# First q and k quad loaded in fp32 over the hardware queues, all of v over GpSimd's queue, bias matmuls apart and one-bank first scores, in a fused attention and channel-mix kernel

## The chip, the cores and the metric

The kernel runs on one core of one Trainium2 chip. The metric is the device time of one execution in microseconds; for the kernel before it is the median of three runs, 227.96 us (227.42 to 228.73). The profile is of a further execution of the same program, which took 229.82 us.

The engines that work beside each other are TensorE (PE, with its weight loads as PEld), VectorE (DVE), ScalarE (ACT), GpSimd (POOL) and SyncE (SP). Each takes its instructions in the order in which they stand in its own list. DMAs are issued by SP and ACT (hardware queues) and by GpSimd (software queue).

## The reference

```python
scores = scale * np.matmul(q, k.transpose(0, 1, 3, 2))   # q, k, v: (8, 8, 576, 64)
rel = pos[:, None] - pos[None, :]
bias = slopes[:, None, None] * (-np.abs(rel).astype(np.float32))[None, :, :]
mask = (rel >= 0) & (rel < window)                       # window = 128
scores = np.where(mask, scores + bias[None], -1000000000.0)
attn = softmax(scores)
x = (attn @ v) with the heads side by side               # (8, 576, 512)
...
xk = mu_k * x + (1.0 - mu_k) * x_prev
xr = mu_r * x + (1.0 - mu_r) * x_prev
k = np.maximum(xk @ w_k, 0.0)                            # w_k: 512 x 1024
v = k * k @ w_v                                          # w_v: 1024 x 512
r = 1.0 / (1.0 + np.exp(-(xr @ w_r)))                    # w_r: 512 x 512
return (r * v).astype(np.float32)
```

`x_prev` is x shifted by one position within a batch. The lines on softmax and on x are shortened here.

## The kernel before

**Attention.** Each of the 8 batches has two *quads* of four heads. A quad of q or k is one load of 128 rows of 1152 values (`quad_load`, into `raw`); DVE transposes it in blocks of 32 x 32 into `qt` (`turn`, L902). `scores4` computes scores of four heads, with keys as rows, in two halves: half 0 holds the first 256 query columns of two key blocks, half 1 the rest (pieces of 256, 192 and 64 columns). Four matmuls of 32 rows each run beside each other (L933). ACT takes the exponential (L954) of two heads at a time, 1024 columns in a double bank of PSUM (`duo`, two of them), into `at`. For batches 1 to 7 DVE multiplies by a prepared mask (L968). For batch 0 the bias and the mask are instead added in PSUM by matmuls of `sid` (a scaled identity per head) with `dist` (L924), in the same planned step as the scores.

`attend` multiplies by v, which has a column of ones for the sum (L668; tiles `vs` and, for the last 64 positions, `tv`); DVE takes the reciprocal (L674) and DVE or ACT scales (L679, L685) into `xu`. For batches 0 to 2 PE transposes `xu` (L706) and ACT copies it to `xt` (L551); from batch 3 on a DMA transpose does this. `shift` forms the two mixes `xk` and `xr` on DVE (L732, L739). Batch 0 goes through attention in two parts (positions 0 to 255, then the rest), so that the channel mix can begin early.

**Channel mix.** For blocks of 256, 384 or 512 positions PE multiplies by `wk_sb` (L797), ACT takes the rectifier (L804), ACT or DVE the square (L768, L770); PE multiplies by `wr_sb` (L815) and ACT takes a tanh in place of the sigmoid (L822); PE multiplies by `wv_sb` (L831), and DVE joins the two and hands the tile to an output DMA (L836, L861). PSUM has, beside the two double banks, four single ones (`uno`), which the mix, the transposes and batch 0's attends share.

**Order.** The whole program is planned as a graph of steps. `Plan.run` goes through it with a duration for each step, and on each engine takes the ready step of lowest rank that gets its buffers. The rank comes from the tables `LEAD`, `SHIFT` and `NUDGE`, which hold numbers found by a search. The order found is then written out as each engine's fixed list.

**The start.** PE runs 90 warming matmuls (L637). SP and ACT each load one block of batch 0's v in fp32 into an output buffer (`v_first`, L544), and ACT and DVE cast one block each (L551). GpSimd's queue takes, in the order of `LOADS`, the first quad of k and q, the forming of `dist`, the second quad of k and q, half of w_k, the rest of v, the other half of w_k, and then batch 1 and the other weights. Its DMAs cast fp32 to bf16 on the way. A transpose waits for its quad; the scores wait for both transposes of their quad; batch 0's first four attends need the first two blocks of v. A one-off transpose on PE (L627) with a copy on DVE (L631) prepares mu.

Of the kernel before, what the change touches and what calls it, by code (L numbers as in the profile page):

```python
# [182 lines left out]
def kernel(  # L183
# [36 lines left out]
    LOADS = 'xyKVkabRcWw'  # L220
    XD = 4
    OTL = 3.5
    VHKB = 327
    BIAS = (0, 1)
    FIN = 384
# [9 lines left out]
    WAIT = 96.32  # L235
# [26 lines left out]
    tv_buf = many(NV, [128, H, W], BF16, "tv")  # L262
    at_buf = many(NA, [128, 2 * 1024 + 64], BF16, "at")
    rc_buf = many(NX, [128, 2, NJ], FP32, "rc")
# [34 lines left out]
    plan = Plan(dict(p2=2, p1=N1, pt=4 - N1, at=NA, xu=NX, vs=NV, cb=NC, qt=NT, xt=2, dl=2, dl0=4,  # L299
# [10 lines left out]
    def dve_t(n, fast=1):  # L310
# [4 lines left out]
        PE: (245.41, 104.68, 82.24, 280.97, 280.85, 383.85, 240.38, 304.14, 232.01, 250.0),  # L315
        ACT: (106.83, 31.51, -1.26, 283.31, -80.09, 110.86, -49.36, -66.59, 49.19, -329.22),
        DVE: (226.97, 54.51, 122.69, 32.62, 2.01, -18.69, -19.49, -68.72, -71.7, 53.31),
# [3 lines left out]
        PE: {(0, 0): 164.1, (3, 0): -101.36, (2, 0): 106.01, (1, 0): -253.38, (1, 1): -8.62, (1, 2): 168.96, ('p1', 'fxk'): -4.58, ('rl', 'fp1'): -124.01, ('frl',): 851.64, ('rs', 'fp1'): 412.51, ('p1', 'fkk'): 3.25, ('fkk',): -221.64, ('ot', 'fp1', 'frs'): -20.61, ('fp1', 'frs'): 251.26},  # L321
        ACT: {(0, 0): -193.01, (3, 0): -156.82, (2, 0): 30.74, (1, 0): -160.97, (1, 1): 250.14, (1, 2): 336.32, ('p1', 'fxk'): 2.22, ('rl', 'fp1'): 331.51, ('frl',): 234.49, ('rs', 'fp1'): -327.51, ('p1', 'fkk'): -152.67, ('fkk',): -200.74, ('ot', 'fp1', 'frs'): -427.51, ('fp1', 'frs'): 310.6},
        DVE: {(0, 0): 106.18, (3, 0): 52.28, (2, 0): 70.04, (1, 0): -243.69, (1, 1): -278.94, (1, 2): 50.14, ('p1', 'fxk'): 976.06, ('rl', 'fp1'): -340.74, ('frl',): 236.08, ('rs', 'fp1'): 888.24, ('p1', 'fkk'): 232.82, ('fkk',): -853.72, ('ot', 'fp1', 'frs'): -155.85, ('fp1', 'frs'): 44.72},
    }
    NUDGE = {
# [210 lines left out]
    def v_first(j, h, deps):  # L536
# [4 lines left out]
        def stage():  # L541
            return ot_buf[hs.idx].rearrange("p (h d) -> p h d", d=D)
# [520 lines left out]
```

## Time and profile before

| | us |
|---|---|
| median of three runs | 227.96 (227.42 to 228.73) |
| profiled execution, device time | 229.82 |
| its span, first to last instruction | 228.0 |
| PE busy in the span | 214.2 |
| DVE busy | 196.6 |
| ACT busy | 163.8 |
| GpSimd busy | 55.1 |

Each row of time order has the start in us, the busy time in us, engine, line, operation, tiles and their shapes; a bracket at the end says how long the engine was idle before and what ended this. Matmuls are pipelined, so a busy time of PE is not work at its peak rate. A DMA shows as the instruction that issues it; its landing is another number.

### The profile page before, as it was taken

What the parts mean: (1) busy time and instruction counts of PE and PEld (TensorE: products, weight loads), DVE (VectorE), ACT (ScalarE), POOL (GpSimd) and SP (SyncE); (2) the same over time, 40 slices, a digit from 0 to 9 for tenths busy, and PEclk for the clock granted to TensorE, in tenths of its full rate; (3) what the DMA queues carried; (4) which work ended last, traced back from release to release, by engine and by line L of the source; (5) the groups of instructions that cost most, each with busy time, mean ns of one, the idle gap of its engine ahead of it and who ended that gap; (6) DMA issues with size and microseconds to landing.
All of it is one profiled execution on the core that took longest, in us unless ns stands there. A gap on an engine that the chain in (4) does not pass through costs nothing.

```text
span 228.0 us, 5641 instructions
## 1 busy us (share of the span) xinstructions
PE 214.2 (94%) x2233; PEld 128.8 (56%) x2263; DVE 196.6 (86%) x376; ACT 163.8 (72%) x313; POOL 55.1 (24%) x85
## 2 busy tenths in 40 slices
PE   8847969999999999999999999999999999999994
PEld 8736647665656555445664555456555446446642
DVE  7856999999999999999999997999697988995332
ACT  6155899988999889596965997847794588417511
POOL 8627445472710000083007400380000000000000
PEclk9997997999999999999999999999999999999999
DMA  7999999999993211489947992699815331422023
GB/s 141 194 181 212 183 176 211 168 212 173 237 169 9 95 46 35 92 190 170 180 95 135 199 187 58 155 183 205 128 40 54 100 138 33 85 97 89 0 92 138
DMA packets 63993, 30.11 MB, mean 132 GB/s; under 512 B 52184, under 2 KB 55776, under 8 KB 63968
## 3 DMA queue, kind: packets, MB, share of 16 engines
q0 software_dynamic: 42672, 16.52, 65.0%
q1 hardware_dynamic: 20112, 12.92, 20.5%
q10 hardware_dynamic: 1184, 0.33, 0.7%
q8 instruction: 17, 0.28, 0.5%
q14 instruction: 8, 0.07, 0.1%
HBM read 33.56 MB, written 9.44 MB: 189 GB/s over the span
## 4 chain that ended last, share of the span: by engine, by line
PE 73%; ACT 10%; DMA 6%; DVE 5%; issue 2%; POOL 1%; POOLq 0%; SPq 0%; DVEq 0%
PE uno L831 25%; PE uno L797 23%; PE uno L815 10%; PE duo L668 7%; PE duo L933 6%; ACT at L954 6%; DMA raw<-in_q_dram 4%; DMA xt<-xu 2%; ACT rl L804 1%; ACT kk L768 1%; PE uno L706 1%; PE duo L924 1%; DVE xr L739 1%; DVE xu L679 1%; DVE at L968 1%
## 5 line engine op out<-in xcount | busy, mean ns | idle before, releaser
L954 ACT ACTIVATE at<-duo 128x1024 bf16<-128x1024 f32 x64 | 64.3, 1041 | 22.9 <-PE duo L933 22.9
L797 PE MATMUL uno<-xk,wk_sb 128*128 128x256 bf16 (+2 forms) x410 | 71.3, 314 | 2.3 <-ACT xt L551 0.8
L831 PE MATMUL uno<-wv_sb,kk 128*128 128x512 bf16 (+2 forms) x286 | 68.1, 373 | 0.7 <-issue 0.2
L804 ACT ACTIVATE rl<-uno 128x256 bf16<-128x256 f32 (+2 forms) x104 | 47.5, 482 | 15.5 <-PE uno L797 13.7
L797 PEld LDWEIGHTS <-wk_sb 128*128 128x128 bf16 x416 | 38.8, 98 | 25.9 <-issue 3.8
L831 PEld LDWEIGHTS <-kk 128*128 128x128 bf16 x296 | 27.8, 98 | 29.3 <-issue 0.9
L902 DVE STREAM_TRANSPOSE qt<-raw 128x576 f32<-128x576 f32 x32 | 38.9, 1239 | 2.6 <-DMA raw<-in_q_dram 1.7
L968 DVE TENSOR_TENSOR at<-at,mask 128x1024 bf16<-128x1024 bf16 x56 | 37.3, 676 | 1.2 <-ACT at L954 0.9
L822 ACT ACTIVATE rs<-uno 128x512 bf16<-128x512 f32 x36 | 22.2, 617 | 19.5 <-PE uno L815 19.5
L815 PE MATMUL uno<-wr_sb,xr 128*128 128x512 bf16 x130 | 35.2, 380 | 0.8 <-issue 0.2
L768 ACT ACTIVATE kk<-rl 128x256 bf16<-128x256 bf16 (+2 forms) x71 | 34.3, 514 | 0.6
L836 DVE SCALAR_TENSOR_TENSOR ot<-rs,uno 128x512 f32<-128x512 bf16 (+2 forms) x37 | 24.2, 661 | 7.2 <-PE uno L831 6.6
L513 POOL DMA_DIRECT2D vs<-in_v_dram x30 | 26.6, 906 | 5.6 <-DMA wv_sb<-in_moe_w_v_dram 2.0
L668 PEld LDWEIGHTS <-at 128*128 128x128 bf16 x576 | 21.9, 100 | 7.9 <-ACT at L954 3.1
L739 DVE SCALAR_TENSOR_TENSOR xk<-dl,mu_sb,xt 128x576 bf16<-128x576 bf16 (+1 forms) x32 | 24.6, 776 | 0.0
L739 DVE SCALAR_TENSOR_TENSOR xr<-dl,mu_sb,xt 128x576 bf16<-128x576 bf16 (+1 forms) x32 | 24.4, 771 | 0.0
L933 PE MATMUL duo<-qt 32*128 32x256 bf16 (+2 forms) x640 | 21.3, 254 | 2.3 <-DVE rc L674 1.1
L679 DVE TENSOR_TENSOR xu<-duo,rc 128x640 bf16<-128x640 f32 x28 | 22.3, 811 | 0.2
L933 PEld LDWEIGHTS <-qt 32*128 32x128 bf16 x640 | 13.8, 94 | 14.3 <-issue 12.6
L815 PEld LDWEIGHTS <-xr 128*128 128x128 bf16 x144 | 13.1, 98 | 14.5 <-issue 1.5
L668 PE MATMUL duo<-vs,at 128*128 128x65 bf16 x448 | 19.3, 197 | 0.5 <-DVE at L968 0.3
L595 POOL COPY gap<-xt 1x4 bf16<-1x4 bf16 x3 | 0.9, 289 | 68.0 <-DMA xt<-xu 68.0
(50 smaller groups left out, 137.4 us busy)
## 6 DMA issues: line engine op xcount, KB each, us to landing
out_dram<-ot SPq DMA_DIRECT2D x32, 256.0 KB, 2.4
raw<-in_k_dram POOLq DMA_DIRECT2D x16, 288.0 KB, 8.3
raw<-in_q_dram POOLq DMA_DIRECT2D x16, 288.0 KB, 7.4
vs<-in_v_dram POOLq DMA_DIRECT2D x30, 128.0 KB, 9.8
wk_sb<-in_moe_w_k_dram POOLq DMA_DIRECT2D x2, 512.0 KB, 12.1
wv_sb<-in_moe_w_v_dram POOLq DMA_DIRECT2D x2, 512.0 KB, 11.3
out_dram<-ot SPq DMA_DIRECT2D x6, 128.0 KB, 1.8
tv<-in_v_dram POOLq DMA_DIRECT2D x8, 64.0 KB, 9.3
```

Of the source, the lines that this page charges most:

```text
L513: return dma(POOL, 256, issue_t(1024), lambda e: nc.gpsimd.dma_start(out=vs_buf[h.idx][:, j, :, 0:D], in_=v[b, :, 128 * j:128 * j + 128].r ...
L668: nc.tensor.matmul(a[:, hl, t - t0], lhsT=at[:, lo:lo + 128], rhs=vs[:, u, 2 * g + hl, :] if u < NF else tvb[:, 2 * g + hl], start=(u == u ...
L739: lambda e: nc.vector.scalar_tensor_tensor(out=buf[hk.idx][:, g, e0 + c0:e0 + c1], in0=dls(), scalar=mu[:, g:g + 1], in1=xc(1), op0=ALU.mu ...
L768: nc.scalar.activation(out=out, in_=in_, func=AF.Square)
L797: nc.tensor.matmul(one(hp)[:, 0:n], lhsT=wk_sb[:, po, 128 * fo:128 * fo + 128], rhs=xk_buf[hx.idx][:, po, c0:c1], start=(po == 0), stop=(p ...
L804: a = op(ACT, act_t(n), [s], pr, lambda e, hp=hp, hr=hr: nc.scalar.activation(out=rl_buf[hr.idx][:, 0:n], in_=one(hp)[:, 0:n], func=AF.Rel ...
L815: nc.tensor.matmul(one(hp), lhsT=xr_buf[hx.idx][:, po, 128 * c:128 * c + 128], rhs=wr_sb[:, po], start=(po == 0), stop=(po == NPO - 1))
L831: nc.tensor.matmul(one(hv)[:, a:b], lhsT=kk_buf[hk.idx][:, fo, o:o + 128], rhs=wv_sb[:, fo, a:b], start=(fo == 0), stop=(fo == NFO - 1))
L902: nc.vector.transpose(out=qt_buf[hq.idx][:, S * i:S * i + S].rearrange("p s t -> p (s t)").bitcast(FP32) .rearrange("p (q t) -> p t q", t=TB),
L933: nc.tensor.matmul(two(hps[j // 2])[:, j % 2, c0:c0 + n], lhsT=qt[r:r + 32, S + 128 * u:S + 128 * u + 128, t], rhs=qt[r:r + 32, q0:q0 + n, t],
L954: lambda e, ah=ah, j=j: nc.scalar.activation(out=ah(), in_=two(hps[j]), func=AF.Exp, scale=float(scale)), (), [hps[j]])
L968: nc.vector.tensor_tensor(out=a, in0=a, in1=m, op=ALU.mult)
```

## The change

It does these things:

- The first quad of k and of q (batch 0, heads 0 to 3) is loaded in fp32, each in two halves of 64 rows, one over SP's and one over ACT's queue, into two `kk` buffers. Each tensor is then cast into `raw` in two halves of 576 columns, one by ACT and one by DVE.
- The first two blocks of v go over GpSimd's queue with the cast in the DMA, like the others. The queue's order is now: second quad of k and q, `dist`, two blocks of v, half of w_k, the rest of v, the other half of w_k, and then as before.
- The bias matmuls of batch 0 are a step of their own, which takes the PSUM banks and can run before q and k are there. Sixteen of them now stand in PE's list ahead of the first scores, eight of these among the warming matmuls.
- The scores of the second quad, first half, go to four single banks, with one exponential of 512 columns for each head in place of two of 1024.
- The reciprocals have six buffers that the plan hands out, in place of four in turn; the memsets of `tv` go by 32-bit elements; the count of hardware DMAs that decides how many of the last output tiles are written in two pieces becomes 63, so that one tile is split in place of three.
- The tables of ranks hold new numbers, so the order on every engine differs. DVE's list has four transposes in a row at the start (k one, k two, q one, q two), and the mask copies behind them. ACT has 18 in place of 12 small scalings of `xu`, and 76 in place of 71 squares.

```diff
-    LOADS = 'xyKVkabRcWw'
+    LOADS = 'ydvKVkabRcWw'
...
+    SINGLE = ((1, 0),)
...
-    rc_buf = many(NX, [128, 2, NJ], FP32, "rc")
+    rc_buf = many(6, [128, 2, NJ], FP32, "rc")
...
-            late(tv_buf[t][64:128], 0.0, 0.55)
+            late(tv_flat[t][64:128].bitcast(FP32), 0.0, 0.34)
...
-        x = dma(eng, VHKB, 0.46, lambda _: e.dma_start(
-            out=stage(), in_=v[0, :, 128 * j:128 * j + 128].rearrange("h p d -> p h d")),
-            [g], lat=(0.7, 0.7), kind="first")
...
+    def first_quads():
+        src = [(q, k)[i][0, 0:4].rearrange("h (p r) d -> (h p) (r d)", r=TB) for i in range(2)]
+        hs = [Hold("kk"), Hold("kk")]
...
+        for i in (1, 0):
+            for n, (eng, e) in enumerate(((SPE, nc.sync), (ACT, nc.scalar))):
+                rows = slice(64 * n, 64 * n + 64)
+                x[i, n] = dma(eng, QUADKB / 2, 0.46, lambda _, i=i, e=e, rows=rows: e.dma_start(
+                    out=stage(i)[rows], in_=src[i][rows]), [last["kk0"]], lat=(0.85, 0.75), kind="first")
+        res = {}
+        for i in (1, 0):
+            res[i] = [op(CAST, {ACT: act_t(TB * D / 2, True), DVE: dve_t(TB * D / 2)}, [x[i, 0], x[i, 1]],
+                         (0, 0, 0, 0, 5), lambda e, i=i, c=c: copy_any(
+                e, raw_buf[ch[0].idx][:, i, 0, c:c + TB * D // 2], stage(i)[:, c:c + TB * D // 2]),
+                (), [hs[i]]) for c in (0, TB * D // 2)]
...
+        elif what == "v":
+            vl[0].extend(v_load(0, j, vh[0], [gv[0]] + blank_v) for j in (0, 1))
...
-    n_hw = 39 + 2 + G * len(XO)
+    n_hw = 39 + 4 + G * len(XO)
...
+        single = b == 0 and (c, half) in SINGLE
+        hps = [Hold("p1") for _ in range(4)] if single else [Hold("p2"), Hold("p2")]
...
+        if bias:
+            deps = deps + [op(PE, 0.02 + sum(4 * mm(n) for _, _, n in pieces),
+                              [n_dist] + n_sid[4 * c:4 * c + 4], prio + (4,), emit_b, hps)]
...
+        for j, js in enumerate(((0,), (1,), (2,), (3,)) if single else ((0, 1), (2, 3))):
```

More of the change, by code (lines that the diff above doesn't have):

```diff
@@ L234 @@
     NO = 6
-    WAIT = 96.32
+    WAIT = 148.12
     COST = {'v': 1.15, 'tv': 0.58, 'w': 0.88}
@@ L314 @@
     LEAD = {
-        PE: (245.41, 104.68, 82.24, 280.97, 280.85, 383.85, 240.38, 304.14, 232.01, 250.0),
-        ACT: (106.83, 31.51, -1.26, 283.31, -80.09, 110.86, -49.36, -66.59, 49.19, -329.22),
-        DVE: (226.97, 54.51, 122.69, 32.62, 2.01, -18.69, -19.49, -68.72, -71.7, 53.31),
+        PE: (412.66, 13.74, 352.24, 231.79, 219.11, 455.43, 521.65, 19.38, 22.83, 259.26),
+        ACT: (120.42, -14.11, -11.49, 9.9, 64.54, -199.58, -184.6, -81.47, -112.35, -120.12),
+        DVE: (540.05, 6.52, 96.4, 66.38, -6.12, -94.16, -131.55, -24.25, 66.99, -77.3),
     }
@@ L442, in fab, with dma @@
         return x
-    def dma(queue, kb, issue, emit, deps=(), need=(), free=(), lat=(1.0, 0.9), flip=False, kind='x'):
+    def dma(queue, kb, issue, emit, deps=(), need=(), free=(), lat=(1.4, 0.9), flip=False, kind='x'):
         n = plan.add(queue, issue, 0.0, list(deps) + [last.get(queue)],
@@ L481 @@
     MSEG = ((256, 192), (448, 64))
+    for e in (PE, ACT, DVE, SPE, POOL):
+        last[e] = plan.add(e, 0.75, 0.0, [], (-1e10,))
     n_warm = dve_op(0.1, lambda e: nc.vector.memset(warm, 0.0), [], (0, -2))
@@ L555 @@
     gv = {0: virtual("vs", [vh[0]])}
-    vl[0] = [v_first(j, vh[0], [gv[0]] + blank_v) for j in range(2)]
+    ch, cl, gc = {}, {}, {}
+    ch[0] = Hold("cb")
+    gc[0] = virtual("cb", [ch[0]])
+    cl[0] = [first_quads()]
+    vl[0] = []
     plan.add(ACT, 1.28, 0.0, [last[ACT]], (-1e9,))
@@ L562, in load_step @@
     def load_step(what):
-        if what in "xy":
-            c = int(what == "y")
-            if c == 0:
-                ch[0] = Hold("cb")
-                cl[0] = []
-                gc[0] = virtual("cb", [ch[0]])
-            cl[0].append({i: quad_load(0, i, c, ch[0], gc[0]) for i in (1, 0)})
-            if c == 0:
-                n_w["d"] = pool_op(0.7, emit_cut, [n_ident])
+        if what == "y":
+            cl[0].append({i: [quad_load(0, i, 1, ch[0], gc[0])] for i in (1, 0)})
+        elif what == "d":
+            n_w["d"] = pool_op(0.7, emit_cut, [n_ident])
+        elif what == "v":
+            vl[0].extend(v_load(0, j, vh[0], [gv[0]] + blank_v) for j in (0, 1))
         elif what == "V":
@@ L603, in batch_load @@
             g_ = virtual("cb", [ch[b]])
-            cl[b] = [[quad_load(b, i, c, ch[b], g_) for i in range(2)] for c in range(2)]
+            cl[b] = [[[quad_load(b, i, c, ch[b], g_)] for i in range(2)] for c in range(2)]
         elif what == "c":
@@ L673, in emit_r @@
         def emit_r(e):
-            nc.vector.reciprocal(out=rc[:, :, 0:nt], in_=a5()[:, :, :, D])
+            nc.vector.reciprocal(out=rc_buf[hr.idx][:, :, 0:nt], in_=a5()[:, :, :, D])
         def emit_x(e):
+            rc = rc_buf[hr.idx]
             out_ = xo().rearrange("p t h d -> p h t d")
@@ L688, in attend @@
         a = op(PE, 0.029 * n_mm, deps, prio + (0,), emit, [hp], [ha, hv])
-        r = op(DVE, 0.2, [a], prio + (0,), emit_r)
+        r = op(DVE, 0.2, [a], prio + (0,), emit_r, [hr])
         on = XU(b, g)
         r = op(on, {ACT: 0.197 * 2 * nt, DVE: dve_t(2 * nt * D)}, [r], prio + (0,), emit_x,
-               [hx], [hp])
+               [hx], [hp, hr])
         return r, hx
@@ L906, in emit @@
                         "p (t w) -> p t w", w=32))
-            n = op(DVE, dve_t(S) + TURN, [cl[b][c][i], (n, 0.0)] + paced(b, 2 * c) + (n_pad if i else []),
+            n = op(DVE, dve_t(S) + TURN, cl[b][c][i] + [(n, 0.0)] + paced(b, 2 * c) + (n_pad if i else []),
                    (0, b, 0, 2 * c, 3), emit, [hq] if i else [], [ch[b]])
@@ L916, in scores4, with bank, emit_b @@
         a0 = BASE[pieces[0][0]] + pieces[0][1] - 128 * pieces[0][0]
-        hps = [Hold("p2"), Hold("p2")]
-        def emit(e):
-            qt = qt_buf[hq.idx]
-            for j in range(4 if bias else 0):
+        single = b == 0 and (c, half) in SINGLE
+        hps = [Hold("p1") for _ in range(4)] if single else [Hold("p2"), Hold("p2")]
+        prio = (0, b, 0, 2 * c + half) if b else (0, 0, half, 2 * c)
+        def bank(j):
+            return one(hps[j]) if single else two(hps[j // 2])[:, j % 2]
+        def emit_b(e):
+            for j in range(4):
                 for (u, q0, n) in pieces:
@@ L924, in emit @@
                     nc.tensor.matmul(
-                        two(hps[j // 2])[:, j % 2, c0:c0 + n], lhsT=sid[:, 4 * c + j],
+                        bank(j)[:, c0:c0 + n], lhsT=sid[:, 4 * c + j],
                         rhs=dist[:, 0:n], start=(u == pieces[0][0]), stop=False,
                         skip_group_check=True)
+        def emit(e):
+            qt = qt_buf[hq.idx]
             for (u, q0, n) in pieces:
@@ L933, in emit @@
                         nc.tensor.matmul(
-                            two(hps[j // 2])[:, j % 2, c0:c0 + n],
+                            bank(j)[:, c0:c0 + n],
                             lhsT=qt[r:r + 32, S + 128 * u:S + 128 * u + 128, t],
@@ L937, in emit, with ah @@
                             start=(t == 0 and not bias), stop=(t == 1), skip_group_check=True)
-        prio = (0, b, 0, 2 * c + half) if b else (0, 0, half, 2 * c)
-        dur = 0.02 + sum(2 * max(n / 2400 + .0025, .03) for _, _, n in pieces)
+        need = (has if half == 0 else []) + ([] if bias else hps)
         if bias:
-            dur += 0.1 + sum(4 * mm(n) for _, _, n in pieces)
-            deps = deps + [n_dist] + n_sid[4 * c:4 * c + 4]
-        s = op(PE, dur, deps, prio + (2,),
-               emit, (has if half == 0 else []) + hps, [hq])
-        s.rows = (128 if bias else 32, 32)
-        res = []
-        for j in range(2):
-            def ah(j=j):
-                return at_buf[has[j].idx][:, 0:2048].rearrange(
-                    "p (h c) -> p h c", h=2)[:, :, a0:a0 + 512]
-            x = op(ACT, act_t(1024), [s], prio + (2,),
+            deps = deps + [op(PE, 0.02 + sum(4 * mm(n) for _, _, n in pieces),
+                              [n_dist] + n_sid[4 * c:4 * c + 4], prio + (4,), emit_b, hps)]
+        s = op(PE, 0.02 + sum(2 * max(n / 2400 + .0025, .03) for _, _, n in pieces), deps, prio + (2,),
+               emit, need, [hq])
+        s.rows = (32, 32)
+        res = [[], []]
+        for j, js in enumerate(((0,), (1,), (2,), (3,)) if single else ((0, 1), (2, 3))):
+            w = 512 * len(js)
+            p = js[0] // 2
+            def ah(js=js, p=p):
+                return at_buf[has[p].idx][:, 0:2048].rearrange(
+                    "p (h c) -> p h c", h=2)[:, js[0] % 2:js[-1] % 2 + 1, a0:a0 + 512]
+            x = op(ACT, act_t(w), [s], prio + (2,),
                    lambda e, ah=ah, j=j: nc.scalar.activation(
-                out=ah(), in_=two(hps[j]), func=AF.Exp, scale=float(scale)), (), [hps[j]])
+                out=ah(), in_=one(hps[j])[:, None] if single else two(hps[j]),
+                func=AF.Exp, scale=float(scale)), (), [hps[j]])
             if bias:
-                res.append(x)
+                res[p].append(x)
                 continue
@@ L968, in emit_m @@
                 nc.vector.tensor_tensor(out=a, in0=a, in1=m, op=ALU.mult)
-            res.append(op(DVE, dve_t(1024, 2), [x, n_mask] + ([] if m0 == 0 else n_mcopy),
+            res[p].append(op(DVE, dve_t(1024, 2), [x, n_mask] + ([] if m0 == 0 else n_mcopy),
                           prio + (2,), emit_m))
@@ L982 @@
             prio = (0, 0, 0, g)
-            r, hx = attend(0, g, 0, 2, has[j], [m0[j]] + vl[0][0:2], prio)
+            r, hx = attend(0, g, 0, 2, has[j], m0[j] + vl[0][0:2], prio)
             xks[0, 0, g], xrs[0, 0, g] = out_t(0, g, 0, 2, hx, [r], prio, xh[0], xth[0], late)
@@ L991 @@
             prio = (0, 0, 1, g)
-            r, hx = attend(0, g, 2, NJ, has[j], [m0[j], m1[j]] + vl[0] + blank, prio)
+            r, hx = attend(0, g, 2, NJ, has[j], m0[j] + m1[j] + vl[0] + blank, prio)
             xks[0, 1, g], xrs[0, 1, g] = out_t(0, g, 2, NJ, hx, [r], prio, xh[0], xth[0])
@@ L1007 @@
                 prio = (0, b, 0, g)
-                r, hx = attend(b, g, 0, NJ, has[j], [m0[j], m1[j]] + vl[b], prio)
+                r, hx = attend(b, g, 0, NJ, has[j], m0[j] + m1[j] + vl[b], prio)
                 if b in XO:
```

29 lines of the change are left out of this document (12 added, 17 removed), and 139 rows, old and new, of the table NUDGE.

## The prediction

> **What bounds the kernel now.** I read the page first, then the busy time by stretch, then the first 27 us in order of time, because the change touches what is loaded and computed there.
>
> ```profile
> span 228.0 us, 5641 instructions
> ...
> PE 214.2 (94%) x2233; PEld 128.8 (56%) x2263; DVE 196.6 (86%) x376; ACT 163.8 (72%) x313; POOL 55.1 (24%) x85
> ```
>
> Busy time by stretch (columns: stretch, its length, busy us of PE, PEld, DVE, ACT and POOL with counts, TensorE clock, DMA share, GB/s):
>
> ```profile
> 12.00:18.00 6.00, 3.27 (x49) 2.26 (x50) 3.02 (x8) 3.54 (x6) 1.76 (x3) 0.92 1.74 184
> 18.00:24.00 6.00, 5.21 (x97) 4.14 (x95) 4.01 (x13) 2.60 (x5) 3.81 (x6) 0.79 1.13 208
> 24.00:30.00 6.00, 4.93 (x77) 3.51 (x79) 6.00 (x13) 6.00 (x13) 2.47 (x4) 1.00 1.98 172
> 30.00:36.00 6.00, 4.46 (x80) 3.29 (x73) 5.48 (x11) 6.00 (x16) 3.47 (x6) 0.84 1.56 193
> 36.00:42.00 6.00, 5.93 (x75) 3.87 (x74) 5.79 (x14) 5.98 (x18) 2.34 (x3) 0.87 1.32 199
> ...
> 60.00:80.00 20.00, 19.65 (x248) 12.33 (x248) 19.74 (x32) 19.16 (x39) 3.74 (x5) 1.00 0.83 111
> ...
> 200.00:216.00 16.00, 15.95 (x99) 9.54 (x99) 10.08 (x24) 8.52 (x19) 0.00 (x0) 1.00 0.18 67
> 216.00:228.00 12.00, 8.91 (x48) 4.32 (x47) 3.59 (x6) 1.19 (x2) 0.00 (x0) 1.00 0.31 109
> ```
>
> From 36 us to the end PE is the bound: 5.93 of 6, 19.65 of 20, 15.95 of 16. Its total work doesn't change, so what it fails to do early is what can be won or lost. Between 12 and 18 us it is busy for 3.27 of 6 us, and ACT for only 3.54: both wait. Between 24 and 36 us ACT is full (6.00 and 6.00) and PE gets 4.93 and 4.46, so there ACT sets the pace. The early rows say what is waited for:
>
> ```profile
> 0.74 0.49 ACTq L544 DMA_DIRECT2D ot<-in_v_dram  x1
> ...
> 4.93 1.80 POOL L513 DMA_DIRECT2D vs<-in_v_dram  x2
> ...
> 5.08 0.62 ACT L551 CAST vs<-ot 128x512 bf16<-128x512 f32 x1
> 5.25 0.86 DVE L551 CAST vs<-ot 128x512 bf16<-128x512 f32 x1
> ...
> 7.87 1.26 DVE L902 STREAM_TRANSPOSE qt<-raw 128x576 f32<-128x576 f32 x1 [0.69 <-DMA raw<-in_k_dram]
> ...
> 8.88 0.22 PE L627 MATMUL uno<-id,mu_row 8*128 8x8 f32 x1
> ...
> 9.27 1.26 DVE L902 STREAM_TRANSPOSE qt<-raw 128x576 f32<-128x576 f32 x1
> ...
> 10.37 0.17 DVE L631 COPY mu_sb<-uno 128x8 f32<-128x8 f32 x1
> 10.58 0.64 PE L933 MATMUL duo<-qt 32*128 32x256 bf16 x16 [0.50 <-DVE mu_sb L631]
> ...
> 10.72 1.26 DVE L902 STREAM_TRANSPOSE qt<-raw 128x576 f32<-128x576 f32 x1 [0.18 <-DMA raw<-in_k_dram]
> ...
> 11.25 1.94 ACT L954 ACTIVATE at<-duo 128x1024 bf16<-128x1024 f32 x2 [4.92 <-PE duo L933]
> ...
> 13.65 1.25 DVE L902 STREAM_TRANSPOSE qt<-raw 128x576 f32<-128x576 f32 x1 [1.68 <-DMA raw<-in_q_dram]
> ...
> 14.96 0.63 PE L933 MATMUL duo<-qt 32*128 32x256 bf16 x16 [1.13 <-DVE rc L674]
> ...
> 15.64 1.94 ACT L954 ACTIVATE at<-duo 128x1024 bf16<-128x1024 f32 x2 [2.46 <-PE duo L933]
> ...
> 17.63 1.87 PE L924 MATMUL duo<-dist,sid 128*128 128x256 bf16 x12 [0.44 <-ACT at L954]
> ...
> 19.43 1.04 PE L933 MATMUL duo<-qt 32*128 32x256 bf16 x24
> ...
> 22.05 1.33 PE L924 MATMUL duo<-dist,sid 128*128 128x256 bf16 x12
> ...
> 23.30 0.64 PE L933 MATMUL duo<-qt 32*128 32x256 bf16 x24
> ...
> 25.50 1.04 ACT L954 ACTIVATE at<-duo 128x1024 bf16<-128x1024 f32 x1
> ```
>
> The four quads (k, q of heads 0-3, then k, q of heads 4-7) come one after the other through GpSimd's queue. Their transposes start at 7.87, 9.27, 10.72 and 13.65, and the scores at 10.58 and 14.96. The bias and scores of the second half (17.63 to 23.94) wait for the two double banks. Batch 0's last exponential ends at 26.54.
>
> **The change part by part: the first quad over the hardware queues.** No row shows contiguous fp32 rows. Nearest are the two v transfers of 256 KB:
>
> ```profile
> ot<-in_v_dram ACTq DMA_DIRECT2D x1, 256.0 KB, 4.3
> ot<-in_v_dram SPq DMA_DIRECT2D x1, 256.0 KB, 3.8
> ```
>
> The four new transfers are 64 x 1152 x 4 = 288 KB each. The k halves leave first, so 0.74 + 3.8 to 4.3, or 4.5 to 5.0; I take 4.7. The q halves come one quad later. A quad costs GpSimd's queue 1.40 and 1.45 (7.87, 9.27, 10.72); so q is in at 6.1. Low bound 5.2 (issued 0.5 later, nothing else); high 8.0 (GpSimd's quads share in equal parts). Each tensor is cast in halves of 576 columns, one on ACT and one on DVE; DVE's took 0.86 for 512, so 0.97, and q is cast at 7.1. k's casts lie in the wait for q.
>
> **GpSimd's queue.** Quad two is now first on it, where k and q landed at 7.87 and 9.27. The hardware queues carry 1152 instead of 512 KB beside it: 640 KB more, at 1.4 us for 576 KB read, 1.6 us. Half of it before quad two is my value: k at 8.7, q at 10.1 (7.9 to 9.4 and 9.3 to 10.9). DVE transposes in a fixed order: k one, k two, q one, q two, so q one stands behind the landing of k two. At 1.25 each: 7.1 to 8.35, 8.7 to 9.95, 11.2, 12.45. Scores one then start at 11.25, 0.7 later than now, and scores two at 12.5, 2.4 earlier. [...]
>
> Both v blocks now follow quad two there: issued at 3.2 and 4.1. The bytes ahead of the second block's end (four quads and two v) are those ahead of q two now, so it lands near 13.65. High bound by the v rows of the first 24 us, 4.1 + 12.0 = 16.1:
>
> ```profile
> DMA to landing us min/median/max: 11.3/12.0/12.4
> ```
>
> The weights keep the same bytes ahead of them; nothing is taken for them.
>
> **One-bank scores, bias apart.** The first bias blocks (8 + 8 matmuls) run in the wait for q and k. Scores two go to four single banks, so nothing waits for the double ones. ACT's order is: heads of quad one, a single bank of quad two, the rest of quad one, three single banks. A 512-column read of PSUM is priced by:
>
> ```profile
> L804 ACT ACTIVATE rl<-uno 128x512 bf16<-128x512 f32 x24 | 14.0, 606 | 6.2 <-PE uno L797 5.6 <-PE uno L815 0.3
> L685 ACT ACTIVATE xu<-uno,rc 128x64 bf16<-128x64 f32 x12 | 2.8, 414 | 0.0
> L768 ACT ACTIVATE kk<-rl 128x256 bf16<-128x256 bf16 x34 | 13.9, 443 | 0.3
> 32.67 1.38 ACT L685 ACTIVATE xu<-uno,rc 128x64 bf16<-128x64 f32 x6
> ```
>
> Exponentials: 11.95 to 12.95; scores two end at 13.15, so 13.15 to 13.75; 14.75; then three at 0.6 to 16.55, against 17.58 now. On PE the mu transpose (0.22) and its copy (0.17) now stand between the scores and the first attend. They need the single bank freed at 13.75, so the first attend starts at 14.3, after v's 13.65. The second half's bias takes 1.33 from 14.75, when the double bank is free; two attends and a transpose later scores start at 16.8 (19.43 now). Their exponentials (17.5 to 20.0 with a copy between) free the banks for the other bias; with a dozen attend matmuls after it, the last scores of batch 0 start at 21.2 (23.30 now): 2.1 earlier. ACT then has three copies and six scalings (1.38) before the last two exponentials, which end at 24.6 (26.54 now): 1.9 earlier.
>
> **The rest.** ACT scales three pieces of xu instead of two (+1.4). Up to batch 1's sixth exponential the new order has three squares fewer on ACT (3 x 0.44 = 1.3). I take these two against each other, 0; if the squares come back at once it costs 1.4. Cheaper tv memsets lie in DVE's wait for k. Two more reciprocal buffers and two output tiles written whole cost nothing, as PE's last matmul ends at 224.4 and the last tile is written as now. The retuned order has 31 instead of 32 blocks of scores on PE; I take 0, with half a microsecond either way.
>
> The sum: lead of 2.1 on PE at the end of batch 0's scores, kept in ACT's stretch (1.9) and then by a PE that is full. The profiled execution took 229.82 with 228.0 in the span, so 1.82 lies around it: 227.7. It ran 1.86 above the median of 227.96, so the forecast is 227.96 - 2.1 = 225.9. Its own range: if q two's and k two's bounds are best, 1.0 more (224.8); if worst, 1.0 less (226.9).
>
> **Rivals.** *ACT hides it (227.8).* For: ACT is at 6.00 of 6.00 from 24 to 36 and 19.16 of 20 from 60 to 80; over the program the new order gives it six more scalings and five more squares. The 1.4 for xu and 0.5 for four single banks (4 x 0.61 against 1.94) eat 1.9 of the 2.1, which leaves 227.8. Against: it idles 4.92 and 2.46 before that, and now starts its flow at 12. Its two casts (0.62 for 512 columns) lie in the first of these idle times.
>
> *GpSimd's queue is late (229.6).* If the fp32 bytes go first throughout, the second v block lands at its bound of 16.1 in place of 14.3. PE stands in order: behind the first attend wait the bias and all later scores, so 1.8 of the 2.1 goes, and with xu and the single banks uncovered (1.4 + 0.5) it is slower by 1.9 - 0.3 = 1.6. It decides from a landing of about 14.3 on; at 16.4 the lead is gone. For: v took 11.3 to 12.4 there. Against: these had a weight ahead of them as well.
>
> *The clock (224.2).* The stretches show 0.92, 0.79, 0.84 and 0.87: PE runs slow for a while around 18 and around 36 us. In the first the twelve bias matmuls took 1.87 instead of 1.33. Each drop misses 1.7 us of full clock: (0.08 + 0.21) x 6 and (0.16 + 0.13) x 6. If a PE kept busier has only one of the two, it gains up to 1.7 more. For: fewer holes at 12 to 18. Against: ACT still paces 24 to 36. [...]
>
> **How the numbers follow.** Main case 0.45, ACT hides it 0.22, GpSimd's queue 0.17, clock 0.16. About 0.5% (1.1 us) is what a measurement can tell from no change. Faster than 226.8: the main case and the clock, less a little at the edge, 0.59; slower than 229.1: the queue and the worse tail of ACT, 0.18; between 0.23. The range from 224.0 to 229.6 reaches the clock's case below and the queue's above, and leaves out their far halves.
>
> **What would show it.** Right: the four transposes back to back from about 7 to 12.5, with no gap over 1 us; first attend by 14.5; the last double-bank scores of batch 0 at 21 to 22; the last exponential of batch 0 near 24.6; PE full from 34. Wrong: a wait of DVE on raw of more than 1 us or of PE on vs; ACT at 6.00 until after 44; PE idle beyond 42 us, which would mean that the retuned order loses what the start wins.

## The result, and the profile after

| | median us | runs | ratio to before, 95% |
|---|---|---|---|
| before, run beside it | 227.69 | 4 | |
| the change | 231.06 (230.89 to 231.20) | 4 | 1.0142 [1.0104, 1.0180] |

The change is 3.4 us slower; forecast were 225.9 and a range up to 229.6. The profiled execution of the kernel after took 231.12. The page's first rows:

```profile
span 229.0 us, 5658 instructions
...
PE 213.3 (93%) x2235; PEld 128.6 (56%) x2263; DVE 193.1 (84%) x371; ACT 169.6 (74%) x327; POOL 57.0 (25%) x85
```

PE has no more work than before (213.3 and 214.2) and a longer span: the loss is idle time. The span of before, 228.0, is that of an execution at 229.82; a further profile of it, below, has 226.6.

Busy time by stretch of the kernel after (columns as in the same view of before):

```profile
12.00:18.00 6.00, 3.52 (x45) 2.46 (x45) 3.82 (x8) 3.41 (x6) 1.96 (x4) 0.63 1.73 180
18.00:24.00 6.00, 5.18 (x94) 4.24 (x92) 3.79 (x14) 4.39 (x13) 3.73 (x5) 0.80 1.14 211
24.00:30.00 6.00, 3.74 (x84) 2.92 (x81) 6.00 (x16) 5.84 (x21) 2.50 (x4) 1.00 1.78 180
30.00:36.00 6.00, 5.14 (x69) 3.51 (x69) 5.96 (x11) 6.00 (x13) 3.32 (x5) 1.00 1.76 172
36.00:42.00 6.00, 5.79 (x69) 4.06 (x69) 5.84 (x13) 6.00 (x15) 2.49 (x4) 1.00 1.14 208
42.00:48.00 6.00, 5.95 (x94) 4.62 (x93) 5.96 (x13) 6.00 (x16) 2.26 (x5) 1.00 2.29 160
...
140.00:160.00 20.00, 18.29 (x202) 9.56 (x204) 17.11 (x30) 13.78 (x20) 7.75 (x10) 1.00 1.01 120
```

Two stretches lose. In the first 30 us PE isn't fuller than before (3.74 of 6 from 24 to 30, where it had 4.93), and the clock from 12 to 18 us is 0.63, where it was 0.92. From 140 to 160 us, in the full part of the program, PE does 18.29 of 20, where before it did 19.84. The row of before:

```profile
140.00:160.00 20.00, 19.84 (x192) 11.12 (x192) 19.06 (x34) 13.12 (x26) 6.55 (x10) 1.00 1.10 169
```

The start, in order of time (rows of other steps left out):

```profile
5.99 0.86 DVE L561 CAST raw<-kk 128x576 bf16<-128x576 f32 x1 [1.25 <-DMA kk<-in_k_dram]
9.61 0.46 DVE L561 CAST raw<-kk 128x576 bf16<-128x576 f32 x1 [2.31 <-DMA kk<-in_q_dram]
9.98 4.49 DVE L912 STREAM_TRANSPOSE qt<-raw 128x576 f32<-128x576 f32 x4
13.45 1.00 PE L950 MATMUL duo<-qt 32*128 32x256 bf16 x16 [2.74 <-DVE qt L912]
14.53 1.04 PE L950 MATMUL uno<-qt 32*128 32x256 bf16 x16
16.79 0.49 PE L677 MATMUL uno<-vs,at 128*128 128x65 bf16 x6 [0.26 <-DVE mu_sb L640]
17.01 1.58 ACT L973 ACTIVATE at<-uno 128x512 bf16<-128x512 f32 x3
17.18 1.86 PE L938 MATMUL duo<-dist,sid 128*128 128x256 bf16 x12
19.52 1.01 PE L950 MATMUL duo<-qt 32*128 32x256 bf16 x24
...
24.05 0.64 PE L950 MATMUL duo<-qt 32*128 32x256 bf16 x24
```

The first q is cast at 9.61; the wait named is the DMA of q. What follows on DVE waits for nothing more: the cast, then four transposes back to back. On PE come scores at 13.45 (10.58 before), first attend at 16.79 (12.33 before), scores of the second half at 19.52 (19.43 before). The DMA issues (KB each, median us from issue to landing) tell what is late:

```profile
kk<-in_k_dram ACTq DMA_DIRECT2D x1, 288.0 KB, 5.2
kk<-in_k_dram SPq DMA_DIRECT2D x1, 288.0 KB, 3.8
kk<-in_q_dram ACTq DMA_DIRECT2D x1, 288.0 KB, 8.2
kk<-in_q_dram SPq DMA_DIRECT2D x1, 288.0 KB, 6.8
```

The loss at 140 us is elsewhere. A wait of DVE in the kernel after (us in total, times, longest), and the order of time there (rows of other steps left out):

```profile
DVE xu L689 <- DMA xt<-xu: 4.2, 3, 2.8
```

```profile
143.24 6.24 SPq L764 DMA_TRANSPOSE xt<-xu  x3
146.10 0.82 DVE L689 TENSOR_TENSOR xu<-duo,rc 128x640 bf16<-128x640 f32 x1 [2.76 <-DMA xt<-xu]
146.98 0.29 PE L950 MATMUL duo<-qt 32*128 32x256 bf16 x2 [0.75 <-DVE xu L689]
```

DVE may not write an `xu` buffer while a DMA transpose still reads it; PE's next scores need the PSUM bank that this scaling frees. Before has no such wait. The one that it has on these DMAs stands a step later, where DVE forms the mixes from `xt`:

```profile
DVE dl L732 <- DMA xt<-xu: 3.3, 3, 2.1
```

There no PSUM bank is held: PE does 19.84 of 20 in that stretch of before.

### The profile page after: what moved, and what is told of

Same layout as the page of the kernel before. It is cut to its first block, busy times and chain, and to the rows that moved or that the text cites. A ratio compares the mean times of both kernels' runs of the same rounds, so it can differ in the third digit from the quotient of the medians.

```text
span 229.0 us, 5658 instructions
## 1 busy us (share of the span) xinstructions
PE 213.3 (93%) x2235; PEld 128.6 (56%) x2263; DVE 193.1 (84%) x371; ACT 169.6 (74%) x327; POOL 57.0 (25%) x85
## 4 chain that ended last, share of the span: by engine, by line
PE 69%; DVE 11%; ACT 9%; DMA 6%; issue 3%; ACTq 0%; DVEq 0%; SPq 0%
PE uno L841 23%; PE uno L807 20%; PE uno L825 11%; PE duo L950 6%; PE duo L677 5%; ACT at L973 4%; DMA kk<-in_q_dram 4%; DVE qt L912 4%; DMA xt<-xu 2%; ACT rl L814 2%; DVE xu L689 1%; DVE xr L749 1%; PE uno L716 1%; DVE at L987 1%; DVE xk L749 1%
## 5 line engine op out<-in xcount | busy, mean ns | idle before, releaser
L973 ACT ACTIVATE at<-duo 128x1024 bf16<-128x1024 f32 x62 | 62.0, 1039 | 20.7 <-PE duo L950 20.7
L807 PE MATMUL uno<-xk,wk_sb 128*128 128x256 bf16 (+2 forms) x411 | 70.1, 313 | 0.8 <-ACT rl L814 0.3
L841 PE MATMUL uno<-wv_sb,kk 128*128 128x512 bf16 (+2 forms) x281 | 65.8, 373 | 1.2 <-issue 0.6
L841 PEld LDWEIGHTS <-kk 128*128 128x128 bf16 x296 | 27.2, 98 | 30.2 <-issue 2.1
L778 ACT ACTIVATE kk<-rl 128x256 bf16<-128x256 bf16 (+2 forms) x76 | 37.5, 523 | 1.0
L912 DVE STREAM_TRANSPOSE qt<-raw 128x576 f32<-128x576 f32 x32 | 38.1, 1240 | 0.0
L515 POOL DMA_DIRECT2D vs<-in_v_dram x32 | 28.4, 909 | 6.4 <-DMA wv_sb<-in_moe_w_v_dram 2.5
L950 PE MATMUL duo<-qt 32*128 32x256 bf16 (+2 forms) x624 | 21.2, 256 | 5.2 <-DVE qt L912 2.7
L950 PEld LDWEIGHTS <-qt 32*128 32x128 bf16 x640 | 14.5, 95 | 16.9 <-issue 13.5
L604 POOL COPY gap<-xt 1x4 bf16<-1x4 bf16 x3 | 2.2, 742 | 71.6 <-DMA xt<-xu 71.6
L677 PE MATMUL duo<-vs,at 128*128 128x65 bf16 x448 | 18.8, 194 | 0.1
```

The lines of the kernel that those rows point to most:

```text
L515: return dma(POOL, 256, issue_t(1024), lambda e: nc.gpsimd.dma_start(out=vs_buf[h.idx][:, j, :, 0:D], in_=v[b, :, 128 * j:128 * j + 128].r ...
L677: nc.tensor.matmul(a[:, hl, t - t0], lhsT=at[:, lo:lo + 128], rhs=vs[:, u, 2 * g + hl, :] if u < NF else tvb[:, 2 * g + hl], start=(u == u ...
L778: nc.scalar.activation(out=out, in_=in_, func=AF.Square)
L807: nc.tensor.matmul(one(hp)[:, 0:n], lhsT=wk_sb[:, po, 128 * fo:128 * fo + 128], rhs=xk_buf[hx.idx][:, po, c0:c1], start=(po == 0), stop=(p ...
L841: nc.tensor.matmul(one(hv)[:, a:b], lhsT=kk_buf[hk.idx][:, fo, o:o + 128], rhs=wv_sb[:, fo, a:b], start=(fo == 0), stop=(fo == NFO - 1))
L912: nc.vector.transpose(out=qt_buf[hq.idx][:, S * i:S * i + S].rearrange("p s t -> p (s t)").bitcast(FP32) .rearrange("p (q t) -> p t q", t=TB),
```

## The experiments

Ratios are to the kernel before, run beside each kernel, with a 95% interval in brackets; they aren't quotients of the medians. "xu in turn" means that the plan hands out the `xu` buffer that has been free longest, in place of the free one of lowest number:

```diff
+        if h.cls == "xu":
+            return min(free, key=lambda a: self.freed.get(a, -4 + a)) if free else None
...
+        if h.cls == "xu":
+            self.turns += 1
+            self.freed[h.idx] = self.turns
```

**Before again.** The kernel before, unchanged.

> The kernel before once more, for a second profile of it. Its first profiled execution (229.82) ran above the other three (227.2 to 228.7). If its early stretch was disturbed (the second quad's q transposed at 13.65, 2.9 after k, where the other steps are 1.4), the second profile has that transpose near 12.2 and a span near 226; then the lead that I worked out against 13.65 was never there. If the profile was typical, the same step is at 13.65 again and the span is near 228.

228.4 us. Its second q is transposed at 12.54 and its second scores start at 13.99; in the profile behind the prediction these were 13.65 and 14.96:

```profile
13.99 1.04 PE L933 MATMUL duo<-qt 32*128 32x256 bf16 x16
...
21.52 0.64 PE L933 MATMUL duo<-qt 32*128 32x256 bf16 x24
```

So the profile that I worked from had a start about 1 us later than this one, and batch 0's last scores 1.8 later (23.30).

**xu in turn, on the change.**

> After, with the four xu buffers handed out in turn (longest free first) in place of the lowest free number; the order of all instructions is the same. Theory flip wait (the loss is made near 142 to 148 us, where VectorE's scaling waits 2.8 us for a DMA transpose that still reads one of two xu buffers used over and over): that wait goes, 1.5 to 2.5 us faster than after, about 229. Theory start (the loss is made before 42 us by the late fp32 q): no change, 231.

228.86, ratio 1.0010 [0.9974, 1.0046]; the wait on xu is gone (PE does 19.74 of 20 from 140 to 160), and the start is as late as with the change (scores one at 13.65). This wait is worth 1.0142 less 1.0010, 1.3%.

**The change with the loads of before.** The hardware queues carry v again, GpSimd the four quads; order, early bias and one-bank scores of the change stay; the last line puts q one's transpose ahead of k two's.

```diff
-                    out=stage(i)[rows], in_=src[i][rows]), [last["kk0"]], lat=(0.85, 0.75), kind="first")
+                    out=vstage(rows.start // 64), in_=vsrc(rows.start // 64)) if i else None, [last["kk0"]], lat=(0.85, 0.75), kind="first")
...
+        steps[ia], steps[ib] = steps[ib], steps[ia]
```

> After, with the loads of before: first quad by GpSimd's queue with the cast in the DMA, two v blocks in fp32 over the hardware queues with two casts; VectorE's order k one, q one, k two, q two. Bias apart, single banks and the whole order stay. Theory start: the scores of the first quad move from 13.45 to about 10.6, those of the second stay near 13.5 to 15, and the time falls by 1 to 2.5 us to 228.5 to 230. Theory flip wait: no change beyond 0.5, 231.

226.98, 0.9941 [0.9901, 0.9980]. Undoing the loads is worth 2.0%, 1.0142 less 0.9941 (the swap of the transposes alone does nothing measurable, below) and takes the kernel from slower to faster than before.

**GpSimd's second quad held back** until the first q has landed, by a small copy on GpSimd ahead of it, so that the hardware queues run alone.

```diff
+                nc.gpsimd.tensor_copy(out=hold, in_=kk_buf[staged[0].idx].rearrange("p f c -> p (f c)").bitcast(FP32)[:, 0:NPO])
```

> After, with GpSimd's queue held (a copy of four columns of the staged q) until the fp32 q has landed, so that the hardware queues have the DMA engines to themselves. If q is late because GpSimd's quads share the engines, q lands near 7.2 to 7.8 in place of 9.6. If the four fp32 halves go one after the other and are themselves slow, q stays at 9 or later. The time is not the point; the second quad comes later, near 13.

One run: 237.57, because the whole of GpSimd's queue is late. Its row is the reading: the four transfers need 7.0 us from issue even with nothing beside them (8.2 in the change).

```profile
kk<-in_q_dram ACTq DMA_DIRECT2D x1, 288.0 KB, 7.0
```

So sharing with GpSimd's quads is only the smaller part of the delay, 1.2 of some 3.5 us.

**Loads of before and xu in turn.**

> Both cures together: the loads of before and the xu buffers in turn; the order of after stays, and so do the early bias and the single banks. If the two losses are separate (4.1 us for the loads, 2.2 for the buffers, by their first runs), the time is 231.06 - 4.1 - 2.2 = 224.8 and below 2% faster than before but clear of it. If they share a part (the run with the loads of before still waited 2.6 us for a DMA transpose), 225.5 to 226.5.

225.82, 0.9908 [0.9886, 0.9931], below both kernels. With the wait on xu gone, undoing the loads is worth 1.0% (1.0010 less 0.9908), half of the 2.0% above.

**34 more warming matmuls**, on the kernel with xu in turn.

```diff
+        for _ in range(35 if len(warmed) == NWARM else 1):
```

> After with the xu buffers in turn, and 34 more warming matmuls between the early bias and the first scores' wait (they compute nothing that is used), so that PE isn't idle from 10.7 to 13.4. Theory clock (part of the price of the late q is that the TensorE clock stands at half from 13.9 to 20.7 in place of 3.4 us): the half-rate stretch shrinks or goes, 0.5 to 1.5 us faster than 228.9. Theory landing alone (ACT's flow of exponentials starts late, whatever PE's clock): the clock changes and the time doesn't, 228.9.

228.32, 1.0027 [1.0005, 1.0049]; by the clock's records it was at half speed for 3.4 us in place of 6.8. The first scores came hardly earlier (13.38), batch 0's last ones at 23.30 for 24.27, and the time doesn't differ clearly from 1.0010 [0.9974, 1.0046].

**The bias matmuls issued with the scores again**, on the kernel with the loads of before and xu in turn; the planned step stays, but issues nothing.

```diff
+            if bias:
+                emit_bias(e)
```

> As the run with both cures, but the bias matmuls are issued together with their scores again, as in before; banks and the rest of the order stay. If the early bias brings what the prediction gave it (about 1.3 us in the second half plus 1.0 in the first), 1 to 2.3 us slower than that run. If PE's wait for the quads hides it anyway, within 0.5 of it.

227.26, 0.9963 [0.9934, 0.9992] against 0.9908 [0.9886, 0.9931]: the early bias is worth some 0.55%, 1.3 us.

**xu in turn on the kernel before.**

> The kernel before with the xu buffers in turn. In its profile no scaling waited for a DMA transpose. So if the wait belongs to the retuned order, no change (227.7 to 228.0); if it is a loss of the allocation in general, 1 us or more faster.

227.72, 0.9990 [0.9963, 1.0016]. It has no wait to lose; the wait belongs to the new order.

**q one transposed ahead of k two**, on the change with xu in turn; the same swap of two planned steps as above.

> The kernel after with xu buffers in turn and only the fixed order of the four transposes changed: k one, q one, k two, q two. Theory (the loads of the first quad are what is late): q one is cast near 9.6 to 9.8 as before this edit, k two lies there by then, so q one's transpose starts near 9.8 or at most 1.3 earlier than its place now; scores one start 1.1 to 1.3 earlier (12.4 instead of 13.65), scores two unchanged (14.5 to 14.7), time 0 to 1.0 us below 228.9. Rival (the place of q one behind k two was the cost): scores one fall to 11.3 or earlier and the time to 227 or below.

228.70, 1.0040 [1.0013, 1.0067]; scores one at 12.23 and scores two at 14.39. The fixed order of the transposes delays the first scores by 1.4. This doesn't show in the time; batch 0's last scores come only 0.2 earlier (24.06 for 24.27).

**Whole tensors**: the first k over SP's queue and the first q over ACT's, 128 rows each, in place of two halves of 64 rows each.

```diff
-                    out=stage(i)[rows], in_=src[i][rows]), [last["kk0"]], lat=(0.85, 0.75), kind="first")
+                    out=stage(i), in_=src[i]) if (i == 1) == (rows.start == 0) else None, [last["kk0"]], lat=(0.85, 0.75), kind="first")
```

> The kernel after with xu buffers in turn; the first k goes whole (128 rows, 576 KB) over SP's queue and the first q whole over ACT's, in place of two halves each. Theory (the fp32 bytes have a common rate, near 230 KB/us beside GpSimd's quads): both end near 8 to 9.6 and k is no longer ahead, so the first cast of k moves from 6.0 to 7 or later, q is cast between 8.6 and 9.8, time 228 to 230. Rival (the halves are what is slow: four transfers of 64 rows in a row): q is in by 7.5, cast by 8.3, scores one start 1.2 or more earlier than 13.65, time 227.5 or below.

224.95, 0.9890 [0.9833, 0.9947]. My theory of a common rate of the fp32 bytes fell. The same 1152 KB are in 5.7 us after their issue, without GpSimd being held:

```profile
kk<-in_q_dram ACTq DMA_DIRECT2D x1, 576.0 KB, 5.7
kk<-in_k_dram SPq DMA_DIRECT2D x1, 576.0 KB, 5.5
```

**Only q over the hardware queues**, k of the first quad first on GpSimd's, with q one's transpose ahead of k two's.

> The kernel after with xu buffers in turn and the transposes in the order k one, q one, k two, q two; of the first quad only q goes in fp32 over the hardware queues (two halves, 576 KB), k goes first on GpSimd's queue, ahead of quad two. Theory (what goes by hardware is paced by its fp32 bytes, 288 KB in 1.2 to 1.4 us): q is in near 5.0 to 5.5 and k near 7.9 as in the kernel before, scores one start at 10.0 to 10.7, scores two at 12.0 to 13.5, the two v blocks land 0.7 to 1.4 later than 12.35, time 225.5 to 227.0. Rival (start of batch 0 does not set the time, the loss lies elsewhere): scores one come 3 us earlier and the time stays within 0.6 of 228.9.

224.66, 0.9872 [0.9832, 0.9913]; scores at 10.52 and 11.31. Both v blocks were in by 11.6, earlier than in the change and not later as I expected.

**Halves by columns**: four transfers again, each 576 columns of all 128 rows.

```diff
+                    out=stage(i)[:, 9 * rows.start:9 * rows.stop],
+                    in_=src[i][:, 9 * rows.start:9 * rows.stop]), [last["kk0"]], lat=(0.85, 0.75), kind="first")
```

> The kernel after with xu buffers in turn; the first k and q still in two halves each over SP's and ACT's queue (four transfers of 288 KB), but each half is 576 columns of all 128 rows in place of all columns of 64 rows. Theory (a transfer into 64 of the 128 partitions is what is slow: 4608 B packets at 300 ns in place of 180): the four transfers are in by 6.0 to 7.0, k cast near 5.0, q cast by 7.5, scores one start at 11.5 or earlier, time 224 to 226. Rival (four transfers in place of two, through two queues, are what is slow): q is cast at 9 or later, scores one start at 13 or later, time 228 to 229.5.

224.04, 0.9873 [0.9806, 0.9940]. It isn't the number of transfers. Their issues, and the start in order of time (rows of other steps left out):

```profile
kk<-in_k_dram ACTq DMA_DIRECT2D x1, 288.0 KB, 4.0
kk<-in_k_dram SPq DMA_DIRECT2D x1, 288.0 KB, 3.8
kk<-in_q_dram ACTq DMA_DIRECT2D x1, 288.0 KB, 4.9
kk<-in_q_dram SPq DMA_DIRECT2D x1, 288.0 KB, 4.5
```

```profile
5.72 0.46 DVE L568 CAST raw<-kk 128x576 bf16<-128x576 f32 x1
6.10 4.81 DVE L919 STREAM_TRANSPOSE qt<-raw 128x576 f32<-128x576 f32 x4
9.89 0.63 PE L957 MATMUL duo<-qt 32*128 32x256 bf16 x16
10.97 0.64 PE L957 MATMUL uno<-qt 32*128 32x256 bf16 x16 [0.45 <-DVE qt L919]
12.78 0.34 PE L684 MATMUL uno<-vs,at 128*128 128x65 bf16 x6 [0.26 <-DVE mu_sb L647]
14.49 0.64 PE L957 MATMUL duo<-qt 32*128 32x256 bf16 x24
```

By the landing records k is in at 4.69 and q at 6.09. All four transposes run back to back from 6.10, and the second half's scores start at 14.49 where the change has 19.52.

**The change itself with whole tensors**, xu as in the change.

> The change itself with one edit: the first k whole over SP's queue, the first q whole over ACT's, in place of two halves of 64 rows each; xu buffers as in the change. Theory (start and xu wait are two losses that add): the start comes as with xu in turn, casts done by 8.5, scores one at 11.1, and the wait on xu near 142 to 148 us stays: time 226 to 228, 3 to 5 us below the change. Rival (the wait on xu depends on how late the program runs there): the wait goes with the late start, time 224.5 to 225.5.

225.91, 0.9940 [0.9900, 0.9980]: 2.0% below the change with that one edit. Scores one, the second half's bias and batch 0's last scores, in order of time, and DVE's wait:

```profile
11.10 0.63 PE L950 MATMUL duo<-qt 32*128 32x256 bf16 x16 [0.68 <-DVE qt L912]
...
14.43 1.04 PE L938 MATMUL duo<-dist,sid 128*128 128x256 bf16 x12
...
19.85 0.64 PE L950 MATMUL duo<-qt 32*128 32x256 bf16 x24
```

```profile
DVE xu L689 <- DMA xt<-xu: 2.5, 2, 1.5
```

The scores are 2.35 earlier than in the change. The wait on xu is shorter and counts less; PE has 19.72 of 20 from 140 to 160.

So it is in part the rival: the two losses don't simply add. The wait is worth 1.3% behind the late start, and 0.5% (0.9940 to 0.9890, overlapping) behind the early one. Seen from the other side, the halves cost 2.0% where the wait stands and 1.2% (1.0010 to 0.9890) where it is gone.

**Halves by odd and even rows**: 64 rows in each transfer, but spread over all 128 partitions.

```diff
+                    out=stage(i)[n:128:2], in_=src[i][n:128:2]), [last["kk0"]], lat=(0.85, 0.75), kind="first")
```

> The kernel after with xu buffers in turn; halves of 64 rows as in the change, but one transfer takes the even and one the odd rows, so that each is spread over all 128 partitions. Theory (writing to one contiguous half of the partitions is slow): like the whole tensors, q cast by 8.5, time 224.5 to 226. Rival (64 rows in a transfer, wherever they go, are slow): casts of q at 9 or later, time 228 to 229.5.

227.34, 1.0004 [0.9971, 1.0036]; q is cast at 8.44, scores one start at 12.27. It lies between, as the issues do:

```profile
kk<-in_k_dram ACTq DMA_DIRECT2D x1, 288.0 KB, 3.3
kk<-in_k_dram SPq DMA_DIRECT2D x1, 288.0 KB, 3.9
kk<-in_q_dram ACTq DMA_DIRECT2D x1, 288.0 KB, 7.1
kk<-in_q_dram SPq DMA_DIRECT2D x1, 288.0 KB, 6.9
```

k comes as fast as with halves by columns (3.3 and 3.9 us from issue, there 4.0 and 3.8). By the landing records q is in at 8.41, against 9.58 in the change and 6.09 with halves by columns. Averages over the trace's packet records of these transfers (first start and last end in us; then, of the mean times of a packet in the first and in the second half of each queue's packets, the lowest and the highest):

```
kernel                   KB a packet   from    to     mean ns
the change                  4.5        2.10   8.57   266 to 322
quad two held back          4.5        2.10   7.66   292 to 329
odd and even rows           4.5        2.10   7.77   183 to 260
whole tensors               4.5        1.77   5.93   183 to 255
halves by columns           2.25       1.77   5.74    93 to 136
```

By the same records the four 64-row halves go one behind the other. With quad two held back, SP's k runs from 2.10 to 3.80, ACT's k from 3.22 to 5.09, SP's q from 4.38 to 6.38 and ACT's q from 5.66 to 7.66.

**The two loads side by side**: halves by columns, and the loads of before, both with the change's order and xu in turn, run beside each other.

> The kernel with halves by columns and xu in turn again, on one chip beside the same order with the loads of before. Theory (the part of the change that moves the loads pays once its transfers cover all 128 partitions): scores one near 9.9, scores of batch 0's second half near 14.5, 2.3 earlier than with the loads of before, 224.0 to 224.6, 1 to 2 us below the other kernel in the same call. Rival (ACT is full from 18 to 42 us and hides an earlier start): within 0.6 us of the other kernel.

> The kernel with the loads of before, the order of the change and xu in turn again, on the same chip. Theory: 225.4 to 226.2, 1 to 2 us above the halves by columns. Rival: within 0.6 us of them.

224.36, 0.9818 [0.9779, 0.9858], beside 226.06, 0.9889 [0.9837, 0.9940]: 1.7 us for the loads. In the earlier runs, not beside each other, the two kernels had 0.9873 and 0.9908, which is 0.8 us with overlapping intervals. In all the first ran 10 times from 223.78 to 226.47, the second 13 times from 224.29 to 228.10. So the change's move of the loads pays once each transfer covers all partitions; by how much is less sure, 0.8 to 1.7 us.

## Why the prediction was wrong

**"The q halves come one quad later ... so q is in at 6.1" is the step that failed.** The mechanism stood, the term was mis-sized by 3.5 us: q was in at 9.58, beyond my high bound of 8.0. I priced a half of 64 rows with the v transfers, which cover 128 partitions, and with GpSimd's time for a quad. The runs show in its place that a transfer into one contiguous half of the partitions needs, alone, some 290 to 330 ns for a packet that takes 183 to 255 when all are covered, and that the four go one behind the other: 1152 KB in 7.66 - 2.10 = 5.6 us alone, against 5.93 - 1.77 = 4.2 us for two whole tensors. These moreover are nearly done when GpSimd's first packet starts (5.12), while q's halves in the change (4.71 to 6.98 and 6.44 to 8.57) share with GpSimd's packets, which start at 4.45 there. Halves of the same 288 KB by columns were in when I had expected it: k at 4.69 and q at 6.09, forecast 4.7 and 6.1. With whole tensors and nothing else changed the kernel takes 225.91, and with xu in turn as well 0.9890 of before; the forecast of 225.9 was 0.991 of 227.96. That these agree is in part luck, as the paragraph on the lead shows.

The packet times (292 to 329 ns with quad two held back, 183 to 255 with whole tensors) and the landings (q in at 9.58 in the change, at 6.09 with halves by columns) go with this, and odd and even rows, which are spread over all 128 partitions, have the short packets (183 to 260). Why a packet into one half of the partitions takes longer isn't shown. The two rows of v that I trusted weren't rows of the same kind.

**GpSimd's queue** came within its bounds, k at the upper one: by the trace's landing records the second k landed at 9.40 and the second q at 10.33 (8.7 and 10.1 forecast, bounds 9.4 and 10.9), and v's second block at 12.35, ahead of the 13.65 I took. So the rival of a late queue had the wrong queue.

**From the cast on the chain was right.** First transpose at 9.98 for 7.1, first attend 16.79 for 14.3, second half's scores 19.52 for 16.8, last ones of batch 0 24.05 for 21.2: each 2.5 to 2.9 late. The sizes on the way differ and partly cancel. Of q's 3.5, the faster cast (0.46 for 0.97) and the transposes without a wait (4.49 us where I had put 5.35, from 7.1 to 12.45) win some 1.4 back; matmuls at the lower clock (the second half's bias took 1.86 for 1.33) lose part of it again. The signs that I had named for a wrong forecast are all there: DVE waits more than 1 us for the DMA of q (2.31), ACT is at 6.00 from 42 to 48 us, where it had 4.96, and PE is idle beyond 42 us. The three single exponentials took 1.58 (1.8 forecast).

**"The retuned order ... I take 0" failed too.** It reuses `xu` buffers whose DMA transposes still run, and costs 1.3% in the change. I counted its blocks of scores and scalings, but did not look at which buffers its order reuses, and how soon.

**The lead was reckoned against one profile**, of an execution that ran 1.86 above the median, and then taken off the median. The last scores of batch 0, from which the lead of 2.1 was counted, start at 23.30 there and at 21.52 in the next profile of the same kernel; against that one the forecast's 21.2 leads by 0.3. The kernel with whole tensors and xu in turn still reached the forecast because its last scores start at 19.92, 1.3 earlier than I had reckoned: two errors cancel there.

**The clock** went against its rival. Of the kernel before, 87 runs have a recorded clock: 48 with 0.995 or more have a median of 227.40, 16 with at most 0.986 one of 229.89. The four runs of the change had 0.976 to 0.984, those of the change itself with whole tensors 0.992 to 1.000. The late start had both the longer idle time of PE (2.74 us ahead of the scores, 0.68 with whole tensors) and the lower clock, so part of the 2.0% for the halves may be the clock. From batch 0's first scores to its last ones the change took 10.60 us (13.45 to 24.05), with 6.8 at half speed by the clock's records, and with whole tensors 8.75 (11.10 to 19.85), at full speed. So of the 4.2 by which the last scores come earlier, 2.35 are the earlier first scores and 1.85 lie behind them; twelve bias matmuls took 1.86 and 1.04. How much of this reaches the time isn't settled: the warming matmuls halved the stretch at the lower clock (3.4 us for 6.8) and changed the time by less than the intervals. That rivals the partitions as the reason for a part of the time, not as the reason for the late landing.

**ACT hides it** is refuted as a whole: the loads side by side give 1.7 us for an earlier start, though ACT is as full from 24 to 42 us (6.00 of 6 in all three stretches, with halves by columns as with the loads of before and xu in turn). It may hide a part, since the second half's scores start 2.3 to 4.2 earlier in the profiles with halves by columns (14.49 and 14.60) than in those with the loads of before (16.80, 18.43 and 18.76).

Right was that the early bias pays. One-bank scores without the early bias, and the new tables apart from the rest, weren't tried.

The best version is the change with halves by columns and xu in turn: 0.9873 and 0.9818 of before in two sets of runs. Only q over the hardware queues (0.9872) and whole tensors (0.9890) don't differ clearly from it.

## What to carry to other kernels

Price a transfer with a row of the same shape on the SBUF side: here a 64-row half was not half of a 128-row transfer (1152 KB took 5.6 us as four 64-row halves alone, 4.2 as two whole tensors). To split one over two queues, try its columns first, with all 128 partitions in each: here that took 5.74 - 1.77 = 4.0 us. When an order or a pool's size changes, look at how soon each buffer is written again after a DMA begins to read it: here one such wait was 2.76 us.

## Not expected of the hardware

- The first issue of a 64-row half took 0.58 us on SP and ACT, that of the same 288 KB over 128 rows 0.40, and ACT's first packets started 1.16 us behind SP's (3.26 and 2.10) in the change, 0.36 behind (2.13 and 1.77) with columns.
- Packets of 2304 B at 93 to 96 ns and of 4608 B at 183, the means of the later ones, carry nearly the same rate (24.0 to 24.8 and 25.2 B a ns), so cutting rows in two cost nothing here.
- Odd and even rows had the short packets (183 to 260 ns), but q was in only at 8.4. Its transfers ran among GpSimd's packets, which start at 3.85 there; why the second pair of 64-row transfers came that late isn't settled.
